# A fused attention and expert kernel: the last block of keys and queries takes another way through PSUM, and its high and low parts are cut in two

## The chip, the cores and the metric

The kernel runs on one core of one Trainium2 chip. The metric is device time in microseconds of one execution, from the first to the last instruction with what lies around them. Engines are named as the profile names them: PE (TensorE matmuls), PEld (its weight loads), DVE (VectorE), ACT (ScalarE), POOL (GpSimd) and SP (SyncE, which issues most DMAs here).

## The reference

Block-causal attention in float32 over 8 batches, 8 heads, 576 positions, head size 64, with blocks of 64 positions; its output, as 4608 tokens of 512 numbers, goes through a two-level router (4 groups of 4 experts, one expert for each token) and the chosen expert's two layers.

```python
def _attn_ref(q, k, v):
    scores = np.matmul(q, k.transpose(0, 1, 3, 2)) / sqrt(64)
    scores = where(pos_q // 64 >= pos_k // 64, scores, -1e9)
    attn = softmax(scores)
    return np.matmul(attn, v)

x = attn_out.transpose(0, 2, 1, 3).reshape(4608, 512)
# router: g = argmax(x @ w_group), e = argmax(x @ w_expert[g]), weight = softmax(g) * softmax(e)
# expert: out[token] = weight * (relu(x @ w1[g, e]) @ w2[g, e])
```

## The kernel before

**Attention.** The work is cut into 32 steps, one for each batch and pair of heads. Step i needs the keys and queries of two heads, turned so that the head size lies on the partitions. `prep` (token K) turns the first 512 positions through PE into a PSUM tile, and `full` (k0, k1, on ACT) copies them into the SBUF tile `nf`, 512 columns for k and 512 for q. The last 64 positions of k and q take three small transposes, `flip_last` (line 175), into a second PSUM tile; `full_last` (j0 for k, 64 columns; j1 for q, 128 columns) copies them behind the others in `nf`, on DVE. Scores are computed in two parts of precision, so `nf` is split: `high` (h0 for k, 576 columns; h1 for q, 640 columns, line 194) rounds it into half 0 of the tile `qk`, and `low` (l0, l1, line 199) subtracts that from `nf` into half 1. h0, h1 and l1 run on POOL, l0 on DVE.

**Scores.** `score` (S0 to S3 and S8, line 228 or 218) multiplies high by high, high by low, low by high, in this order. S2 of step i is the first of its step; it does S0's work too, and reads the first 512 columns of k and q alone. S8 is the one that reads the last columns. `rowmax` (D) takes the maxima on DVE, `expo` (E) the exponentials on ACT, `trans` (T) transposes them on PE, t drains these, `values` (V, line 313) multiplies by the values into the PSUM tile `o`, and v on DVE copies that out. All these PSUM tiles come from one pool of four, taken in turn.

**Order.** Every engine runs its instructions in the order in which the program issues them, and that order is written out by hand as the string `ORDER`: one pass over it is a period, and `S2@0` means S2 of step x in period x, `j0@-1d` means j0 of step x+1, on DVE (a: ACT or POOL). In the kernel before, V of step x-2 also takes the three small transposes of step x+1 into its own PSUM tile `o`, behind its products. In the string V is the 21st of 60 tokens, j0, j1, h0, v, D1, l0, D8 and then h1, l1 follow, and S2 of the next step is the third token of the next period. In the first eight periods five further places in the order (one after every 12 tokens) take a DMA issue on POOL: the odd periods use the first, third and fifth, the even ones the second and fourth.

**Experts.** After the attention come the experts, 14 slots with loaded weights and the tokens gathered by index (lines 927 to 1170). `store` scales each finished tile of outputs by the routing weight and scatters its rows into the output by an indirect DMA on POOL (line 1167). In the last slot of the order the scaling is shared: 256 columns on ACT (line 1160), 256 on DVE (line 1161). Behind all slots stands a loop, `overflow` (line 1342), over a count `cnti` that is zero when no expert has more tokens than planned; all engines load the count and test it. The count is written by DVE in `spill` (line 646), at about 519 us.

Of the kernel before, what the change touches and what calls it, by code (L numbers as in the profile page):

```python
# [50 lines left out]

ORDER, ON_DVE = parse("""
Z2@7 E3@1 S2@0 D2@0 Z4@8 E2@1 n1@3a E8@1 T1@1 t3@1a t1@1a D0@0 K@-1 Z0@10 Y1@4 S3@0 D3@0 G2@6 R0@3
k0@-1a V@2 k1@-1a E0@0 E4@0 E5@0 E1@0 M1@4 E6@0 T2@1 S1@0 L0@3 E7@0 t2@1a T4@1 Z3@8 G1@5 S8@0 G0@4 j0@-1d G4@6
j1@-1d t0@1a Z1@9 h0@-1a v@2d L1@2 D1@0 l0@-1d D8@0 n0@3a G3@6 X0@4 X1@5 Y0@3 h1@-1a t4@1a M0@3 l1@-1a T3@0
X2@6
""")

# [9 lines left out]
class Attention:  # L68
# [99 lines left out]

    def flip_last(self, i, ps):

        x = self.lds[i]["k"]
        for z, n in ((0, 0), (1, 0), (1, 1)):
            r = slice(64 * z, 64 * z + 64)
            o = 384 * z + 64 * n
            self.nc.tensor.transpose(out=ps[:, z, o:o + 64], in_=x[r, 8 + 2 * n:10 + 2 * n, :].rearrange("p a d -> p (a d)"),
                                     identity=self.c["ident"][r, r])

# [5 lines left out]
    def full_last(self, i, n):  # L183
        r = self.rs[i]
        w = 64 + 64 * n
        self.evac(("j", n), r["nf"][:, S * n + 512:S * n + 512 + w], r["jps"][:, n, 384 * n:384 * n + w], 0.125 if n else None)

    def side(self, tok):
        return self.nc.vector if tok in self.on_dve else self.nc.gpsimd

    def high(self, i, n, eng=None):
        r = self.rs[i]
        o = slice(S, 2 * S + BLK) if n else slice(0, S)
        (eng or self.side(("h", n))).tensor_copy(r["qk"][:, 0, o], r["nf"][:, o])  # L194

    def low(self, i, n, eng=None):
        r = self.rs[i]
        o = slice(S, 2 * S + BLK) if n else slice(0, S)
        (eng or self.side(("l", n))).tensor_tensor(out=r["qk"][:, 1, o], in0=r["nf"][:, o], in1=r["qk"][:, 0, o].bitcast(F32),  # L199
                                              op=ALU.subtract)  # L200

    PROD = ((0, 0), (0, 1), (1, 0))

    def score(self, i, u):
        nc = self.nc
        r = self.rs[i]
        b, pr = divmod(i, 4)
        if b not in self.sms:
            self.sms[b] = self.small.tile([P, 4, 2, NT], F32, tag="sm", name=f"sm{b}")
            nc.gpsimd.memset(self.sms[b], 1.0)  # L210
        if "nm" not in r:
            r["nm"] = self.small.tile([P, NB], F32, tag="nm", name=f"nm{i}")
        t = r["qk"]
        ps = self.wide(f"s{i}_{u}")
        if u == 8:
            for h in range(2):
                for x, (hq, hk) in enumerate(self.PROD):
                    nc.tensor.matmul(ps[:, h, 0:288], lhsT=t[:, hq, S + 512:S + 512 + P],  # L218
                                     rhs=t[:, hk, 288 * h:288 * h + 288], start=x == 0, stop=x == 2)
            r["s", u] = ps[:, :, 0:288]  # L220
            return
        for u, c0 in ((2, 0), (0, 384)) if u == 2 else ((u, 0),):
            w = P * (u + 1)
            st = r["s", u] = ps[:, :, c0:c0 + w]
            for x, (hq, hk) in enumerate(self.PROD):
                for z in range(2):
                    p = slice(64 * z, 64 * z + 64)
                    nc.tensor.matmul(st[:, z, :], lhsT=t[p, hq, S + P * u:S + P * u + P], rhs=t[p, hk, 0:w],  # L228
                                     start=x == 0 and c0 == 0, stop=False)
        m = 2 if u == 0 else 1  # L230
        for z in range(2):
            p = slice(64 * z, 64 * z + 64)
            o = ps[:, z, c0 + w - P * m:c0 + w].rearrange("p (n c) -> p n c", c=P)[:, :, BLK:]
            nc.tensor.matmul(o, lhsT=self.mq[p, :], rhs=self.mk[p, 0:m, :], start=False, stop=True)  # L234

    def rowmax(self, i, u):
        r = self.rs[i]
# [52 lines left out]
    def values(self, i, N):  # L290
        nc = self.nc
        o = self.wide(f"o{i}")
        if i + 3 < N:
            self.rs.setdefault(i + 3, {})["jps"] = o
        if i >= 0:
            self.products(i, o)
        if i + 3 < N:
            self.flip_last(i + 3, o)

    def products(self, i, o):  # L300
        nc = self.nc
# [22 lines left out]
    def start(self, N, order, on_dve, init):  # L324
        nc = self.nc
        self.load(0)
        self.wsb = self.pb[0][:, 0:256].bitcast(BF16)
        nc.vector.memset(self.wsb, 0.0)
        self.wps = self.wide("wps")[:, 0, :]
        self.warm(7)  # L330
        if N > 1:
            self.load(1)
        init()
        self.clear()
        self.on_dve = set()
        self.prep(0)
        self.on_dve = {("k", 1), ("j", 1)}
        self.values(-3, N)
        for n in range(2):
            self.full(0, n)  # L340
            self.full_last(0, n)
        self.on_dve = on_dve
        self.warm(5)
        self.high(0, 0, nc.vector)
        self.high(0, 1)
        self.low(0, 0, nc.vector)
        self.low(0, 1, nc.vector)
        if N > 2:
            self.load(2)

# [18 lines left out]

    def token(self, i, tok, N):  # L370
        k = tok[0]
        if not (-2 if k == "V" else k in "Kkjhl") <= i < N:
            return
        if k == "S":
            self.score(i, tok[1])
        elif k == "D":
            self.rowmax(i, tok[1])
        elif k in "tv":
            self.drain(i, tok)
        elif k == "E":  # L380
            self.expo(i, tok[1])
        elif k == "T":
            self.trans(i, tok[1])
        elif k == "V":
            self.values(i, N)
        elif k == "K":
            self.prep(i)
        elif k == "k":
            self.full(i, tok[1])
        elif k == "j":  # L390
            self.full_last(i, tok[1])
        elif k == "h":
            self.high(i, tok[1])
        elif k == "l":
            self.low(i, tok[1])
        elif i % 4 == 3:
            self.router.token(self, i // 4, tok)

# [7 lines left out]
R = 64  # L406
# [18 lines left out]
class Router:  # L425
# [184 lines left out]
        self.res = res  # L610
        yield

    def spill(self, at, row, cnti):
        nc = self.nc
        V = nc.vector
        ts, tt, stt = self.ts, self.tt, self.stt
        one = [R, 1]
        x = tt(self.res[:, 1:2], self.cap, ALU.subtract, sh=one)
        xi = self.t(one, I32)
        ts(x, 0.0, ALU.max, P // UNIT - 1.0, ALU.add, out=xi)  # L620
        xi = ts(xi, (P // UNIT).bit_length() - 1, ALU.arith_shift_right, sh=one, dt=I32)
        ov = self.t(one)
        V.tensor_copy(ov, xi)
        st = stt(self.cap, float(UNIT), self.res[:, 2:3], ALU.mult, ALU.add, sh=one)
        rhs = self.t([R, 4, R])
        ts(self.trif, ov[:, 0:1], ALU.mult, out=rhs[:, 0:2, :])
        ts(self.c["ident"][0:R, 0:R], self.res[:, 0:1], ALU.mult, out=rhs[:, 2, :])
        ts(self.c["ident"][0:R, 0:R], st[:, 0:1], ALU.mult, out=rhs[:, 3, :])
        yield
        ps = at.psT("spill")  # L630
        nc.tensor.matmul(ps[0:R, 0:4 * R], lhsT=self.onesf, rhs=rhs.rearrange("p c r -> p (c r)"),
                         start=True, stop=True)
        yield
        g = self.t([R, 4, R])
        V.tensor_copy(g, ps[0:R, 0:4 * R].rearrange("p (c r) -> p c r", r=R))
        lo = ts(g[:, 1, :], self.pid[:, 0:1], ALU.is_le, sh=[R, R])
        ind = stt(g[:, 0, :], self.pid[:, 0:1], lo, ALU.is_gt, ALU.mult, sh=[R, R])
        stt(g[:, 1, :], -128.0, g[:, 3, :], ALU.mult, ALU.add, out=g[:, 3, :])
        ts(g[:, 3, :], self.p128[:, 0:1], ALU.add, out=g[:, 3, :])
        yield  # L640
        prod = tt(g[:, 2:4, :], ind.unsqueeze(1).broadcast_to([R, 2, R]), ALU.mult, sh=[R, 2, R])
        res = self.red(prod, sh=[R, 2])
        col = self.t([R, 2], I32)
        V.tensor_copy(col, res)
        nc.sync.dma_start(row, col)
        V.tensor_copy(cnti[0:1, 0:1], g[0:1, 0, R - 1:R])
        yield

    def token(self, at, b, tok):
# [193 lines left out]
class Moe:  # L843
# [302 lines left out]
    def store(self, s, c, full):  # L1146
# [10 lines left out]
                nc.vector.scalar_tensor_tensor(out=tmp[0:n], in0=y[z:z + n], scalar=cw[z:z + n], in1=src[0:n],  # L1157
                                               op0=ALU.mult, op1=ALU.add)
        elif s.get("o") == len(self.slots) - 1:
            nc.scalar.activation(ys[0:n, 0:256], y[0:n, 0:256], AF.Copy, scale=cw[0:n])  # L1160
            nc.vector.tensor_scalar(out=ys[0:n, 256:512], in0=y[0:n, 256:512], scalar1=cw[0:n], scalar2=None, op0=ALU.mult)
        elif c % 2 == 0:
            nc.vector.tensor_scalar(out=ys[0:n], in0=y[0:n], scalar1=cw[0:n], scalar2=None, op0=ALU.mult)  # L1163
        else:
# [197 lines left out]
def attention_moe(ctx, tc, q, k, v, w_group, w_expert, w1, w2, out, order=None, on_dve=None):  # L1362
# [16 lines left out]
    with tc.manual_schedule(engines={ET.PE, ET.Activation, ET.DVE, ET.Pool, ET.SP}):  # L1379
# [52 lines left out]
            6: [lambda: b("X", 4), lambda: moe.getids(slots[1])],  # L1432
            7: [moe.grow_raw],
        }
        spl = ro.spill(at, rowo, cnti)
        for n in (60, 63, 65, 67, 68, 69):
            hooks[n] = [lambda: next(spl, None)]
        run = moe.run(hooks)
# [21 lines left out]
        b("G", 1)  # L1460
        for _ in run:
            pass
    moe.overflow(cnti, rowo)


# [24 lines left out]
```

## Time and profile before

| what | us |
| --- | --- |
| median of three runs | 786.62 (786.08 to 788.21) |
| the profiled execution, its own time | 785.75 |
| span of that execution in the profile | 784.0 |
| attention, from the start to about | 322 |
| PE busy over the span | 759.1 |

The span is what the instruction records cover; the profiled execution's own time has 1.75 us more around it. The profile's views used below are its page, the list of waits, the timeline of one engine in a stretch, the groups of instructions by line and shape, and the view of one source line. A line of a timeline gives the start in us, the duration in us, the engine, the line of the program, the operation, the tiles (out<-in), the shape, and in brackets how long the engine had been idle and what ended that.

### The profile page before, as it was taken

How to read it: one execution, taken by the hardware profiler on the slowest of the kernel's cores; microseconds unless marked ns; L12 is line 12 of the kernel's file. 1: busy time of each engine (PE TensorE's matmuls, PEld its weight loads, DVE VectorE, ACT ScalarE, POOL GpSimd, SP SyncE). 2: the span in 40 equal slices, each digit the busy share in tenths (PEclk: the TensorE clock that was granted, in tenths of full speed). 3: DMA queues.
4: the chain of work that ended last, by engine and by line, in shares of the span. 5: the costliest groups of instructions: out<-in, count | busy, mean ns of one | idle time of the engine just before them, and what ended most of it. 6: DMA issues, size and time to landing. Idle time of an engine off the chain costs nothing.

```text
span 784.0 us, 20180 instructions
## 1 busy us (share of the span) xinstructions
PE 759.1 (97%) x7422; PEld 620.5 (79%) x7422; DVE 544.7 (69%) x1153; ACT 500.4 (64%) x1244; POOL 350.2 (45%) x481
## 2 busy tenths in 40 slices
PE   7899999999999999999999999999999999999996
PEld 4677777777777787768888788788988888888874
DVE  5567888888888888885454654754666667777742
ACT  5999999999999998755433433432434545545622
POOL 6444345454545454344143644454551553544212
PEclk9999999999999999999999999999999999999999
DMA  6478464646464636443779979979778897787771
GB/s 137 96 210 237 116 137 109 139 109 139 108 139 108 140 102 159 166 123 117 271 203 225 365 228 237 287 223 219 245 200 234 267 268 188 204 250 231 261 245 42
DMA packets 219108, 146.71 MB, mean 187 GB/s; under 512 B 155558, under 2 KB 186870, under 8 KB 219008
## 3 DMA queue, kind: packets, MB, share of 16 engines
q1 hardware_dynamic: 209920, 120.76, 57.6%
q0 software_dynamic: 9088, 24.64, 9.9%
q8 instruction: 60, 0.98, 0.5%
q14 instruction: 40, 0.33, 0.1%
HBM read 113.46 MB, written 24.59 MB: 176 GB/s over the span
## 4 chain that ended last, share of the span: by engine, by line
PE 80%; ACT 7%; DVE 6%; issue 3%; POOL 2%; DMA 2%; POOLq 0%; SPq 0%; ACTq 0%; DVEq 0%
PE h L1050 18%; PE y L1114 18%; PE o L313 10%; PE s L228 7%; PE tp L157 6%; PE h L1043 4%; PE s L218 3%; ACT pb L251 3%; PE ye L1114 3%; ACT pt L284 3%; PE he L1050 3%; PE y L1122 2%; DVE wl L949 1%; PE y L1133 1%; PE lg L690 1%
## 5 line engine op out<-in xcount | busy, mean ns | idle before, releaser
L1050 PE MATMUL h<-xt,wh 128*128 128x264 f32 (+6 forms) x704 | 156.3, 312 | 2.4 <-DVE xt L1010 2.3
L251 ACT ACTIVATE pb<-s,nm 128x128 f32<-128x128 f32 (+4 forms) x288 | 156.1, 568 | 3.5 <-DVE nm L239 1.6
L949 DVE TENSOR_TENSOR wl<-raw,wh 128x512 fp32r<-128x512 f32 x192 | 147.3, 804 | 8.5 <-ACT wh L948 8.4
L239 DVE TENSOR_REDUCE nm<-s 128x2 f32<-128x768 f32 (+4 forms) x160 | 126.3, 806 | 34.1 <-PE s L234 29.9
L1050 PEld LDWEIGHTS h<-xt,wh 128*128 128x128 f32 x704 | 119.2, 188 | 18.2 <-issue 4.2
L948 ACT CAST wh<-raw 128x512 fp32r<-128x512 f32 x192 | 109.6, 618 | 8.6 <-DMA raw<-in_moe_w_dram 6.0
L284 ACT COPY pt<-tp 128x1024 f32<-128x1024 f32 (+4 forms) x160 | 105.3, 696 | 8.6 <-PE tp L157 6.4
L1050 PE MATMUL h<-xt,wl 128*128 128x264 f32 (+6 forms) x352 | 109.2, 310 | 0.0
L1114 PE MATMUL y<-wh,hring 128*128 128x512 f32 x306 | 106.9, 400 | 0.4 <-ACT ys L1165 0.2
L228 PE MATMUL s<-qk 64*128 64x384 f32 (+3 forms) x768 | 89.9, 343 | 6.4 <-POOL qk L199 3.0
L1167 POOL DMA_INDIRECT out_dram<-ys,ids x40 | 47.0, 1174 | 108.1 <-DVE ys L1163 88.3
L313 PE MATMUL o<-pt,vb 128*64 128x320 f32 (+4 forms) x896 | 93.6, 360 | 0.4 <-DVE tmp L708 0.2
L194 POOL CAST qk<-nf 128x640 fp32r<-128x640 f32 (+1 forms) x63 | 42.7, 701 | 98.1 <-DVE nf L281 71.4
L313 PEld LDWEIGHTS o<-pt,vb 128*64 128x64 f32 x896 | 59.3, 137 | 32.2 <-DVE tmp L708 0.3
L157 PE MATMUL tp<-ident,pb 64*128 64x64 f32 x1600 | 76.3, 226 | 1.6 <-DVE xT L281 1.1
L228 PEld LDWEIGHTS s<-qk 64*128 64x128 f32 x768 | 61.6, 188 | 15.0 <-POOL qk L199 6.1
L157 PEld LDWEIGHTS tp<-ident,pb 64*128 64x128 f32 x1600 | 63.8, 140 | 10.2 <-ACT pb L251 3.9
L982 POOL COPY pl<-xg 128x1024 int16<-128x1024 int16 (+3 forms) x35 | 40.3, 1154 | 62.3 <-DMA xg<-xd,ids 40.6
L1114 PEld LDWEIGHTS y<-wh,hring 128*128 128x128 f32 x306 | 57.4, 188 | 13.1 <-DVE hring L1061 0.5
L1050 PEld LDWEIGHTS h<-xt,wl 128*128 128x128 f32 x352 | 66.2, 188 | 1.2
L251 ACT ACTIVATION_READ_ACCUMULATOR pb<-s,nm 128x1 f32 x288 | 64.1, 223 | 0.0
L199 POOL TENSOR_TENSOR qk<-nf,qk 128x640 fp32r<-128x640 f32 x31 | 61.2, 1975 | 2.6
(255 smaller groups left out, 1324.0 us busy)
## 6 DMA issues: line engine op xcount, KB each, us to landing
raw<-in_moe_w_dram SPq DMA_DIRECT2D x96, 512.0 KB, 4.2
rawq<-in_moe_w_dram SPq DMA_DIRECT2D x24, 512.0 KB, 7.8
natk<-in_k_dram SPq DMA_DIRECT2D x32, 256.0 KB, 3.6
natq<-in_q_dram SPq DMA_DIRECT2D x32, 256.0 KB, 5.5
vb<-in_v_dram SPq DMA_DIRECT2D x64, 128.0 KB, 2.8
wh<-in_moe_w_dram SPq DMA_DIRECT2D x16, 512.0 KB, 5.0
xd<-xns SPq DMA_DIRECT2D x12, 512.0 KB, 3.2
tab<-fill POOLq DMA_DIRECT2D x10, 512.0 KB, 4.1
```

Source lines behind the costliest of these rows:

```text
L157: self.nc.tensor.transpose(out=out[:, z], in_=src[r], identity=self.c["ident"][r, r])
L199: (eng or self.side(("l", n))).tensor_tensor(out=r["qk"][:, 1, o], in0=r["nf"][:, o], in1=r["qk"][:, 0, o].bitcast(F32), op=ALU.subtract)
L228: nc.tensor.matmul(st[:, z, :], lhsT=t[p, hq, S + P * u:S + P * u + P], rhs=t[p, hk, 0:w], start=x == 0 and c0 == 0, stop=False)
L239: self.nc.vector.tensor_reduce(out=o, in_=r["s", u], op=ALU.max, axis=ax, negate=True)
L251: nc.scalar.activation(reg, src, AF.Exp, bias=r["nm"][:, t:t + 1], accum_out=self.sms[b][:, pr, z, u:u + 1])
L284: return self.nc.scalar.copy(dst, src)
L313: nc.tensor.matmul(o[64 * a:64 * a + 64, hf, c0:c0 + BLK * (b1 - t)], lhsT=r["v"][:, a, j, :], rhs=pt[:, PTJ * j + t:PTJ * j + b1, a, :], ...
L948: nc.scalar.copy(h[:, sl], s["raw", u][:, sl])
L949: nc.vector.tensor_tensor(out=l[:, sl], in0=s["raw", u][:, sl], in1=h[:, sl].bitcast(F32), op=ALU.subtract)
L1050: nc.tensor.matmul(o, lhsT=ww[:, dc, f], rhs=rr[:, dc, t], start=dc == 0 and x == 0, stop=dc == 3 and x == 2)
L1114: nc.tensor.matmul(y[c][0:n], lhsT=hh, rhs=w, start=k == 0 and x == 0, stop=k == 7 and x == 2)
L1167: i = nc.gpsimd.indirect_dma_start(out=self.out, out_offset=bass.IndirectOffsetOnAxis(ap=s["ids"][0:n, c, 0:1], axis=0), in_=ys[0:n], in_o ...
```

## The change

- V no longer takes the three small transposes. S1 of step x takes those of step x+1, behind its own products, into columns 256 to 383 of each half of its score tile, which S1 (256 columns wide) leaves unused. For the first step they go into a tile of their own.
- high and low are cut into the first 512 columns and the last ones (kt, 64 columns of k; qt, 128 columns of q). h0 is now one instruction over the first 512 columns of k and of q together (1024 columns), right behind k1 in the order. h1 is two small ones, kt and qt. l0 is low of k's first 512 columns, on DVE; l1 is low of q's first 512 columns, on POOL; a new l2 is low of kt and qt, on POOL.
- In the order, j0 and j1 stand behind D1 instead of ahead of v; h1 stands right behind them, then l0 and D8; l1 keeps its place and l2 comes two tokens behind it.
- In the last slot ACT scales all 512 columns. The count of the overflow loop is copied into `cnti` by POOL at the very end of the experts' work instead of by DVE in `spill`.

```diff
-k0@-1a V@2 k1@-1a E0@0 E4@0 E5@0 E1@0 M1@4 E6@0 T2@1 S1@0 L0@3 E7@0 t2@1a T4@1 Z3@8 G1@5 S8@0 G0@4 j0@-1d G4@6
-j1@-1d t0@1a Z1@9 h0@-1a v@2d L1@2 D1@0 l0@-1d D8@0 n0@3a G3@6 X0@4 X1@5 Y0@3 h1@-1a t4@1a M0@3 l1@-1a T3@0
+k0@-1a V@2 k1@-1a h0@-1a E0@0 E4@0 E5@0 E1@0 M1@4 E6@0 T2@1 S1@0 L0@3 E7@0 t2@1a T4@1 Z3@8 G1@5 S8@0 G0@4 G4@6
+t0@1a Z1@9 v@2d L1@2 D1@0 j0@-1d j1@-1d h1@-1a l0@-1d D8@0 n0@3a G3@6 X0@4 X1@5 Y0@3 l1@-1a t4@1a M0@3 l2@-1a T3@0
...
+        self.rs.setdefault(i, {})["jps"] = ps
...
-            o = 384 * z + 64 * n
+            o = 256 + 64 * n
...
+    def part(self, t, n):
+
+        if n == "kq":
+            return t[:, 0:2 * S].rearrange("p (n c) -> p n c", c=S)[:, :, 0:512]
+        return t[:, dict(k=slice(0, 512), q=slice(S, S + 512), kt=slice(512, S), qt=slice(S + 512, 2 * S + BLK))[n]]
...
+        eng.tensor_copy(self.part(r["qk"][:, 0], n), self.part(r["nf"], n))
...
+        eng.tensor_tensor(out=self.part(r["qk"][:, 1], n), in0=self.part(r["nf"], n),
+                          in1=self.part(r["qk"][:, 0], n).bitcast(F32), op=ALU.subtract)
...
+        if u == 1 and i + 1 < self.N:
+            self.flip_last(i + 1, ps)
...
-        if i + 3 < N:
-            self.rs.setdefault(i + 3, {})["jps"] = o
-        if i >= 0:
-            self.products(i, o)
-        if i + 3 < N:
-            self.flip_last(i + 3, o)
+        self.products(i, o)
...
-            self.high(i, tok[1])
+            for n in ("kt", "qt") if tok[1] else ("kq",):
+                self.high(i, n, self.side(tok))
         elif k == "l":
-            self.low(i, tok[1])
+            for n in (("k",), ("q",), ("kt", "qt"))[tok[1]]:
+                self.low(i, n, self.side(tok))
...
-        V.tensor_copy(cnti[0:1, 0:1], g[0:1, 0, R - 1:R])
+        self.over = g[0:1, 0, R - 1:R]
...
-            nc.scalar.activation(ys[0:n, 0:256], y[0:n, 0:256], AF.Copy, scale=cw[0:n])
-            nc.vector.tensor_scalar(out=ys[0:n, 256:512], in0=y[0:n, 256:512], scalar1=cw[0:n], scalar2=None, op0=ALU.mult)
+            nc.scalar.activation(ys[0:n], y[0:n], AF.Copy, scale=cw[0:n])
...
+        nc.gpsimd.tensor_copy(cnti, ro.over)
     moe.overflow(cnti, rowo)
```

## Rows read from the trace of the kernel before

**Rows 1.** The page: busy us (share of the span) and instructions of each engine.
```profile
PE 759.1 (97%) x7422; PEld 620.5 (79%) x7422; DVE 544.7 (69%) x1153; ACT 500.4 (64%) x1244; POOL 350.2 (45%) x481
```

**Rows 2.** The list of waits, whole span: us in total, times, longest us.
```profile
PE s L228 <- POOL qk L199: 3.0, 4, 1.0
...
PEld s L228 <- POOL qk L199: 6.1, 13, 1.3
```

**Rows 3.** Timeline of DVE, 198 to 203 us: j0, j1, v, D1, l0.
```profile
198.72 0.23 DVE L281 COPY nf<-o 128x64 f32<-128x64 f32 x1 [0.18 <-PE o L175]
198.86 0.28 DVE L282 TENSOR_SCALAR nf<-o 128x128 f32<-128x128 f32 x1
199.06 0.75 DVE L281 COPY xT<-o 128x576 f32<-128x576 f32 x1
199.72 0.68 DVE L239 TENSOR_REDUCE nm<-s 128x2 f32<-128x512 f32 x1
200.32 0.75 DVE L199 TENSOR_TENSOR qk<-nf,qk 128x576 fp32r<-128x576 f32 x1
```

**Rows 4.** Timeline of POOL, the same stretch: h0 and h1 (merged), l1.
```profile
199.08 1.32 POOL L194 CAST qk<-nf 128x576 fp32r<-128x576 f32 x2 [0.49 <-DVE nf L281]
200.49 1.99 POOL L199 TENSOR_TENSOR qk<-nf,qk 128x640 fp32r<-128x640 f32 x1
```

**Rows 5.** Timeline of PE, the same stretch: T4 begins, S1 ends, S8, S2.
```profile
199.41 0.25 PE L157 MATMUL tp<-ident,pb 64*128 64x64 f32 x1
199.43 0.20 PE L234 MATMUL s<-mk,mq 64*128 64x64 bf16 x1
...
199.95 1.03 PE L218 MATMUL s<-qk 128*128 128x288 f32 x6
...
202.01 1.25 PE L228 MATMUL s<-qk 64*128 64x384 f32 x12
```

**Rows 6.** Timeline of POOL, then of PE, 109.5 to 114.8 us: l1, T4, S8, S2.
```profile
111.68 2.11 POOL L199 TENSOR_TENSOR qk<-nf,qk 128x640 fp32r<-128x640 f32 x1
...
111.40 0.53 PE L157 MATMUL tp<-ident,pb 64*128 64x64 f32 x10
111.85 1.05 PE L218 MATMUL s<-qk 128*128 128x288 f32 x6
...
113.86 1.06 PE L228 MATMUL s<-qk 64*128 64x384 f32 x12
```

**Rows 7.** Timeline of all engines, 20 to 26 us: an l1 and the l0 that overlaps it.
```profile
22.47 1.54 POOL L199 TENSOR_TENSOR qk<-nf,qk 128x640 fp32r<-128x640 f32 x1
...
23.09 1.53 DVE L199 TENSOR_TENSOR qk<-nf,qk 128x576 fp32r<-128x576 f32 x1
```

**Rows 8.** Groups by line and shape, POOL, 0 to 320 us: xcount | busy us, mean ns | idle before.
```profile
L194 POOL CAST qk<-nf 128x576 fp32r<-128x576 f32 x31 | 20.6, 664 | 96.3 <-DVE nf L281 71.4 <-ACT pb L251 24.9
...
L667 POOL COPY ry<-rx 128x20 f32<-128x20 f32 x14 | 2.3, 195 | 26.7 <-DVE rx L664 26.7
```

**Rows 9.** Timeline of POOL, 51 to 56 us: an early period, between h0 and h1.
```profile
52.34 0.53 POOL L515 DMA_DIRECT2D tab<-fill  x1
```

**Rows 10.** Timelines at the end: ACT 766 to 769 us, then all engines from 775 us.
```profile
767.83 0.69 ACT L1165 ACTIVATE ys<-y,ids 128x512 f32<-128x512 f32 x1 [1.51 <-DVE ys L1163]
...
776.97 0.47 ACT L1160 ACTIVATE ys<-y,ids 128x256 f32<-128x256 f32 x1 [4.94 <-PE y L1114]
778.02 0.48 DVE L1161 TENSOR_SCALAR ys<-y,ids 128x256 f32<-128x256 f32 x1 [5.27 <-ACTq L1342]
778.79 0.99 POOL L1167 DMA_INDIRECT out_dram<-ys,ids  x1 [5.81 <-DVE ys L1161]
```

**Rows 11.** Lines 1342 and 1486: xcount: duration ns min/median/max, first and last start us.
```profile
L1342 PEldq EVENT_SEMAPHORE  x13: 51/51/51, 777.0 to 778.7; - x13
L1342 POOLq INC_SWDGE_SEM  x1: 943/943/943, 773.5 to 773.5; - x1
...
L1486 POOLq DRAIN  x3: 46/115/4631, 778.6 to 783.7; - x3
```

More of the change, by code (lines that the diff above doesn't have):

```diff
@@ L185, in full_last, with high, low @@
         w = 64 + 64 * n
-        self.evac(("j", n), r["nf"][:, S * n + 512:S * n + 512 + w], r["jps"][:, n, 384 * n:384 * n + w], 0.125 if n else None)
+        self.evac(("j", n), r["nf"][:, S * n + 512:S * n + 512 + w], r["jps"][:, n, 256:256 + w], 0.125 if n else None)
     def side(self, tok):
         return self.nc.vector if tok in self.on_dve else self.nc.gpsimd
-    def high(self, i, n, eng=None):
+    def part(self, t, n):
+        if n == "kq":
+            return t[:, 0:2 * S].rearrange("p (n c) -> p n c", c=S)[:, :, 0:512]
+        return t[:, dict(k=slice(0, 512), q=slice(S, S + 512), kt=slice(512, S), qt=slice(S + 512, 2 * S + BLK))[n]]
+    def high(self, i, n, eng):
         r = self.rs[i]
-        o = slice(S, 2 * S + BLK) if n else slice(0, S)
-        (eng or self.side(("h", n))).tensor_copy(r["qk"][:, 0, o], r["nf"][:, o])
-    def low(self, i, n, eng=None):
+        eng.tensor_copy(self.part(r["qk"][:, 0], n), self.part(r["nf"], n))
+    def low(self, i, n, eng):
         r = self.rs[i]
-        o = slice(S, 2 * S + BLK) if n else slice(0, S)
-        (eng or self.side(("l", n))).tensor_tensor(out=r["qk"][:, 1, o], in0=r["nf"][:, o], in1=r["qk"][:, 0, o].bitcast(F32),
-                                              op=ALU.subtract)
+        eng.tensor_tensor(out=self.part(r["qk"][:, 1], n), in0=self.part(r["nf"], n),
+                          in1=self.part(r["qk"][:, 0], n).bitcast(F32), op=ALU.subtract)
     PROD = ((0, 0), (0, 1), (1, 0))
@@ L337, in start @@
         self.on_dve = {("k", 1), ("j", 1)}
-        self.values(-3, N)
+        self.N = N
+        self.flip_last(0, self.wide("jp"))
         for n in range(2):
@@ L343, in start @@
         self.warm(5)
[L344 to L347, printed above, removed]
+        self.high(0, "k", nc.vector)
+        self.high(0, "q", nc.gpsimd)
+        self.low(0, "k", nc.vector)
+        self.low(0, "q", nc.vector)
+        for n in ("kt", "qt"):
+            self.high(0, n, nc.gpsimd)
+        for n in ("kt", "qt"):
+            self.low(0, n, nc.gpsimd)
         if N > 2:
@@ L371, in token @@
         k = tok[0]
-        if not (-2 if k == "V" else k in "Kkjhl") <= i < N:
+        if not 0 <= i < N:
             return
@@ L611, in final, with spill @@
         yield
-    def spill(self, at, row, cnti):
+    def spill(self, at, row):
         nc = self.nc
@@ L1434, in attention_moe @@
         }
-        spl = ro.spill(at, rowo, cnti)
+        spl = ro.spill(at, rowo)
         for n in (60, 63, 65, 67, 68, 69):
```

## The prediction

> **What bounds the kernel now.** The page comes first: PE is busy for 759.1 of 784.0 us [rows 1], so anything that does not make PE wait less, or do less, moves little. The change takes no work from PE: the three small transposes go from V to S1, one for one. What is left is the 25 us in which PE waits, and the list of waits says which of them the change can touch. PE waits for the low part of q from POOL (l1) 17 times in 31 periods: 13 times as a weight load, 6.1 us in all, and 4 times as a matmul, 3.0 us [rows 2]. All other changes of the attention touch waits of tenths.
>
> Then the timelines of one period show why l1 is late. DVE copies j0 and j1 at 198.72 and 198.86, then v, D1 and l0 [rows 3]. POOL runs h0 and h1 from 199.08 to 200.40 and l1 from 200.49 to 202.48 [rows 4]. S2 of the next step starts at 202.01, and its third product is the first that needs l1 [rows 5]. Its twelve matmuls take 1.25 us there, against 1.06 us in a period where l1 was done before S2 began, at 113.79 against 113.86 [rows 6]. So PE and POOL are nearly balanced: in 13 of the later periods l1 comes out just too late and costs PE up to 0.19 us, in the others it has about 0.4 us in hand (the first four matmuls need no l1). A period repeats through this chain: S2 waits for l1, the rest of PE's period follows, and out of it come the next transposes. Whatever l1 loses in those 13 periods, the kernel loses each time.
>
> The end of the kernel is the second place: ACT's half of the last scaling starts at 776.97, DVE's half only at 778.02, after ACT's part of the overflow loop's test, and the last scatter at 778.79 [rows 10].
>
> **The chain of l1, before and after.** The anchor is D1, which waits for the end of S1. S1's last matmul ends at 199.63 [rows 5]; D1 starts at 199.72, right behind v [rows 3]. Without the transposes PE gets to S1 about 0.15 us sooner, an estimate from ten transposes in 0.53 us [rows 6], and at its end it spends about that again on them. The tracking of PSUM goes by tile, so D1 waits for them too: I put its start 0.04 us earlier, no more. v is done by then, 0.5 us sooner than now. So D1 stays where it is, and j0 and j1, which ran ahead of it, now run behind it.
>
> Before, from D1's start to l1's end: 202.48 - 199.72 = 2.76 us.
>
> After, counted from D1's start: j0 at 0.60 (as l0 followed D1, 199.72 to 200.32), j1 at 0.74 (0.14 behind j0), l0 at 0.94 (0.20 behind j1, as v was) [rows 3]. l0 has 512 columns in place of 576: 0.75 x 512 / 576 = 0.67, to 1.61. kt needs j0 to have landed, qt needs j1: j0's end at 198.95 was followed by h0 at 199.08 [rows 3, 4], so kt can start at 0.95 and meets l0.
>
> Here the two engines hinder each other. Where l1 ran first, alone, it took 1.54 us, and l0, started in the middle of it at 23.09, ended at 24.62, 0.62 us behind l1's end at 24.01: it took 1.53 us in place of 0.75 [rows 7, 3]. Where l0 ran first, to 201.07, l1 took 1.99 us and ended 1.41 us behind it [rows 3, 4]. One waits for the other's end, and only its start-up, some 0.13 us, is hidden. The Trainium skill has this as a rule (SBUF — State Buffer, Who interferes with whom): VectorE with two SBUF inputs and a GpSimd instruction that reads SBUF exclude each other for a whole instruction, and the one that starts first goes first. The rows agree, 1.99 against 1.54 us; by the rule alone the order of kt and l0 here is open, since both could start at about 0.95.
>
> The prices of kt and qt are in no row. Below them stands a copy of 20 columns, 195 ns; above them h0's 576 columns, 664 ns [rows 8]. Between the two lies 0.84 ns a column, so kt is 0.23 us and qt 0.29 us. Behind l0 kt adds 0.10 (its start is hidden), qt 0.24 (POOL's instructions overlap by 0.05). l1 has 512 columns: 1.41 x 0.8 + 0.13 = 1.26, less 0.05 of overlap, 1.21. Its end: 1.61 + 0.10 + 0.24 + 1.21 = 3.16. GPSIMD Engine Reference of the Trainium skill (Elementwise — side-by-side cycle accounting) gives 4497 ns for 2048 columns of such an instruction, from which I estimate 1.12 us for l1; by that the sum below would be lower by 16 x 0.14 = 2.2 us, and no row has that size.
>
> So l1 ends 3.16 - 0.04 - 2.76 = 0.36 us later than now. It is shorter by 128 columns and h0 is out of its way, but it had been behind l0 and not behind h0 all along, and l0 and the small high parts now start behind D1 and both copies. Bounds: if kt, qt, l0 and l1 did not hinder each other at all, l1 would end at 1.02 (j1's end) + 0.13 + 0.24 + 1.26 = 2.65, which is 0.15 earlier than now. If l0 came last, behind kt, qt and l1, it would end at 2.65 + 0.62 = 3.27; S2's second product needs it about 0.15 before the third needs l1, so PE would wait for it as if l1 were 0.65 later.
>
> **The sum.** 13 periods x 0.36 = 4.7 us. Of the four waits as a matmul, all in the first periods, I count three at the same 0.36, 1.1 us; the first of them falls in step 0, where PE has other waits beside it, and I take 0 (0.36 more if they do not cover it). A DMA issue of 0.53 us that stood between h0 and h1 in the even early periods [rows 9] now stands, by the order, between h1 and l1, so it delays l1 as before. The other 11 later periods have their 0.4 us in hand and lose nothing.
>
> h0 over 1024 columns costs POOL about 0.2 + 0.84 x 1.0 = 1.04 us, right behind k1. Its result is needed by S2 of the next step, after V, T2, S1, T4, S8 and T3, and POOL is idle in most of that time (busy 350.2 of 784.0 us [rows 1]), so it costs nothing; without that cover it would be 1 us. l2, some 0.7 us, comes behind l1 and is needed by S8 half a period on: nothing. v ends 0.5 us sooner, and S8, which started 0.14 us behind v's end and 0.54 behind T4's first transpose, 0.45 where v is not in its way [rows 3, 5, 6], gains up to 0.09; in the 13 periods l1 decides anyway, elsewhere I take 0.4 us in all off. At the start the low part of q is 128 columns shorter on DVE: 0.1 off. Moving the next loads behind S1 delays only transfers that are needed more than a period later: nothing.
>
> The end: ACT's whole scaling takes 0.69 (as at 767.83), to 777.66, and 0.28 later, as now, the scatter starts: 777.94 in place of 778.79, 0.85 sooner [rows 10]. But POOL's copy of the count now stands behind that scatter's issue of 0.99, and every engine's test of the loop behind the copy. PE's part of the test took from 777.0 to 778.7, and POOL has a step of 0.94 in its own [rows 11]; all of that lay beside the last scaling and would now come after 779.0, up to about 782.7. The last drain on POOL ended at 783.2 (778.55 + 4.63) [rows 11], so it ends between 0.85 us earlier (if it hangs on the scatter alone) and 2.9 us later (if its 3.4 us behind the scatter's issue come after the test). I take 0.2 off, because the test fits in what the drain waits for now.
>
> Together: 4.7 + 1.1 - 0.4 - 0.1 - 0.2 = 5.1 us. The profiled execution took 785.75 us, 1.75 more than its span, and lies 0.87 below the median of 786.62. On the median this is 791.7 us.
>
> **Rivals.** (a) l0 comes last on its port: kt starts a moment before l0 and POOL keeps its turn. For it speaks that kt and l0 become ready within 0.02 us; against it that l0 came on right behind the one POOL instruction that held it up, with 0.62 us left [rows 7]. 13 x 0.65 + 3 x 0.65, and about 0.1 in the 11 others: 786.6 + 11 = 798 us. (b) Faster: kt and qt slip through ahead of l0 without holding it or l1 up, and l1 ends 0.15 us earlier. It decides from the point where l1 ends less than 2.76 us behind D1. Then 13 x 0.15 = 2.0, three early ones 0.5, S8 up to 0.8, 0.3 at both ends: 783.0 us. For it speaks that POOL's chain gets 1.3 us of h0 and h1 off; against it that j0 and j1 come 1.6 us later. (c) The change does not do what it is for, and nothing shows: kt and qt cost half of what I think, l1 ends within 0.1 of now, and PE's time for a period decides: 786 to 788 us. (d) The loop's test at the end sets the time, with the chain as forecast: 791.7 + 3 = 794.8 us.
>
> **How the numbers follow.** Measurements here tell differences from about 0.3%, 2.4 us, so "same" is 784.3 to 789.0. Chances: forecast 0.45, (d) with it 0.08, (a) 0.12, (c) 0.19, (b) 0.16. Faster is (b), 0.16; same is (c), with 0.02 of the forecast's lower tail, 0.21; slower the rest, 0.63. The forecast's own range, with l1 at 2.2 us less or kt and qt twice as dear, is 789 to 795. The 8 in 10 leave out half of (b) below and some of (a) above: 783.6 to 797.
>
> **What would show it.** In the profile after, per period: l0 on DVE about 0.3 us later against D1; POOL with one cast of about 1.0 us behind k1 and two small ones around l0; l1 about 1.3 us long, its end some 3.1 us behind D1's start. PE's wait for l1 at S2 in more than 17 periods, and 10 us or more in all. Period lengths up by 0.3 to 0.4 in the two of four that are short now, unchanged in the others. At the end, the scatter at about 1 us behind PE's last matmul, and all engines' tests of the loop behind it. I am wrong if l1 ends less than 2.8 us behind D1, if D1 itself moves, or if S2 is seen waiting for l2, which its first 512 columns do not need.

## The result, and the profile after

The median went from 787.07 us (five runs, 786.08 to 788.21) to 792.66 us (five runs, 791.60 to 795.52): 1.0077 times the time before, with a 95% interval of 1.0055 to 1.0099. The kernel became slower by 5.6 us; the forecast was 791.7 us, with a range of 783.6 to 797.0. The profiled execution took 791.6 us and its span 789.9 us, 5.85 us more than the span before.

The page of the kernel after, busy us and instructions of each engine, against [rows 1]:

```profile
PE 757.4 (96%) x7422; PEld 617.5 (78%) x7422; DVE 546.5 (69%) x1151; ACT 502.6 (64%) x1244; POOL 370.0 (47%) x579
```

PE does the same 7422 matmuls, so the added time is PE's waiting or lies behind PE. POOL has 98 instructions and 20 us more. The list of waits says what PE waits for, against [rows 2]:

```profile
PEld s L233 <- POOL qk L204: 14.6, 20, 1.9
...
PE s L233 <- POOL qk L204: 8.3, 18, 1.6
```

S2's weight loads wait for the low part of q 20 times in place of 13 and 8.5 us longer, and its matmuls 18 times in place of 4, in the same periods, 5.3 us longer. One short period shows why. DVE's timeline after, 161 to 166 us (v, D1, j0, j1, l0, D8), against [rows 3]:

```profile
160.82 0.76 DVE L288 COPY xT<-o 128x576 f32<-128x576 f32 x1
162.06 0.69 DVE L246 TENSOR_REDUCE nm<-s 128x2 f32<-128x512 f32 x1 [0.48 <-PE s L176]
162.67 0.21 DVE L288 COPY nf<-s 128x64 f32<-128x64 f32 x1
162.80 0.28 DVE L289 TENSOR_SCALAR nf<-s 128x128 f32<-128x128 f32 x1
163.00 0.73 DVE L204 TENSOR_TENSOR qk<-nf,qk 128x512 fp32r<-128x512 f32 x1
163.65 0.74 DVE L246 TENSOR_REDUCE nm<-s 128x1 f32<-128x576 f32 x1
```

POOL's timeline, the same stretch (kt and qt as one row; l1 and the two parts of l2 as one), against [rows 4]:

```profile
162.95 0.93 POOL L200 CAST qk<-nf 128x64 fp32r<-128x64 f32 x2 [2.21 <-DVE nf L288]
163.85 1.96 POOL L204 TENSOR_TENSOR qk<-nf,qk 128x512 fp32r<-128x512 f32 x3
```

PE's timeline, the same stretch (S8, and S2 in two pieces), against [rows 5, 6]:

```profile
162.26 1.05 PE L223 MATMUL s<-qk 128*128 128x288 f32 x6
...
164.29 0.61 PE L233 MATMUL s<-qk 64*128 64x384 f32 x4
165.18 0.72 PE L233 MATMUL s<-qk 64*128 64x384 f32 x8 [0.27 <-POOL qk L204]
```

D1 waits 0.48 us for S1's tile, now with the small transposes in it; j0 and j1 follow, then l0. Of the merged row of POOL the single records give kt from 162.95 to 163.18, qt from 163.14 to 163.88, 0.15 behind l0's end, and l1 from 163.85 to 165.12. So l1 ends 3.06 us behind D1's start, 0.30 later than the 2.76 before. PE's third product waits for it and goes on 0.06 behind it. From V's start l1 ends at 7.27 us in place of 6.99, and the short periods are longer by just that, 0.28 us.

Groups of POOL by line and shape, 0 to 322 us, in the kernel after (count, busy us, mean ns, idle before), against [rows 8]:

```profile
L204 POOL TENSOR_TENSOR qk<-nf,qk 128x512 fp32r<-128x512 f32 x31 | 39.4, 1271 | 0.0
L200 POOL CAST qk<-nf 128x1024 fp32r<-128x1024 f32 x31 | 32.1, 1036 | 35.4 <-ACT nf L292 35.4
L200 POOL CAST qk<-nf 128x128 fp32r<-128x128 f32 x32 | 23.7, 740 | 0.0
...
L200 POOL CAST qk<-nf 128x64 fp32r<-128x64 f32 x32 | 8.6, 268 | 72.0 <-DVE nf L288 72.0
```

The end, in a timeline of all engines after 775 us, against [rows 10]:

```profile
780.09 0.69 ACT L1169 ACTIVATE ys<-y,ids 128x512 f32<-128x512 f32 x1 [4.94 <-PE y L1123]
781.05 0.99 POOL L1175 DMA_INDIRECT out_dram<-ys,ids  x1 [4.95 <-ACT ys L1169]
782.03 0.18 POOL L1471 CAST cnti<-fin 1x1 int32<-1x1 f32 x1
```

and in the views of the lines of the loop and of the end (count, ns min/median/max, first and last start), against [rows 11]:

```profile
L1349 POOLq TENSOR_LOAD <-cnti x1: 773/773/773, 782.2 to 782.2; - x1
...
L1350 POOLq INC_SWDGE_SEM  x1: 975/975/975, 783.4 to 783.4; - x1
...
L1495 POOLq DRAIN  x3: 46/109/3257, 785.8 to 789.6; - x3
```

All engines load the count at 782.2, behind its copy, and POOL's last step of the test starts at 785.6. Only then does POOL's drain begin, and it takes 3.26 us of its own, though the scatter's instruction had ended at 782.04, 3.7 us before. Before, the drain began at 778.55 and ran beside the scatter.

Where the 5.85 us lie, by the starts of V's products (from one to the next is a period) and the end of PE's last matmul. From the sixth on, the periods come in fours: two short ones, one of a third kind and one of a fourth.

| stretch | before | after | difference |
| --- | --- | --- | --- |
| start to the first V | 28.69 | 27.83 | -0.86 |
| the first five periods | 49.17 | 50.41 | +1.24 |
| 12 short periods (9.32 before, 9.60 after) | 111.88 | 115.26 | +3.38 |
| 6 periods of the third kind (10.2; 10.1) | 61.25 | 60.59 | -0.66 |
| 5 periods of the fourth kind (10.4) | 52.46 | 53.36 | +0.90 |
| the last three | 25.15 | 25.16 | 0.0 |
| last V to PE's last matmul | 448.33 | 447.45 | -0.88 |
| PE's last matmul to the end | 7.09 | 9.82 | +2.73 |

The first row and the last but one are not put down to the change, since kernels with the same code there differ by as much: the first V starts at 28.69 to 29.59 in the kernel before and in experiments 2 and 8, at 27.83 and 28.82 in the kernel after and in experiment 1, and the stretch from the last V to PE's last matmul is 447.5 to 451.7 us over the ten profiles of this study.

Of the +0.90 of the fourth kind 0.60 lies in one period, which took 10.93 us before and 11.53 after. POOL's timeline there in the kernel after, then DVE's:

```profile
270.03 1.05 POOL L200 CAST qk<-nf 128x1024 fp32r<-128x1024 f32 x1
...
270.16 0.94 DVE L539 TENSOR_TENSOR fin<-fin,eb 64x16 f32<-64x16 f32 x1
```

The router's small addition ends 0.02 us behind h0, and v stands behind it on DVE. Before, with POOL idle there, it took 0.15 us. All seven kernels of this study with h0 over 1024 columns show 0.94 us there, the three with the old h0 0.15.

### The profile page after: what moved, and what is told of

Its sections match the earlier page's. It is cut to its first block, busy times and chain, and to the rows that moved or that the text cites. A ratio compares the mean times of both kernels' runs of the same rounds, so it can differ in the third digit from the quotient of the medians.

```text
span 789.9 us, 20222 instructions
## 1 busy us (share of the span) xinstructions
PE 757.4 (96%) x7422; PEld 617.5 (78%) x7422; DVE 546.5 (69%) x1151; ACT 502.6 (64%) x1244; POOL 370.0 (47%) x579
## 4 chain that ended last, share of the span: by engine, by line
PE 75%; ACT 8%; DVE 7%; POOL 5%; issue 3%; DMA 1%; SPq 0%; DVEq 0%; ACTq 0%
PE h L1059 19%; PE y L1123 18%; PE o L315 11%; PE s L233 7%; PE tp L157 6%; PE h L1052 4%; ACT pt L291 3%; PE ye L1123 3%; ACT pb L258 3%; POOL qk L204 3%; PE he L1059 3%; PE y L1131 2%; POOL qk L200 2%; DVE wl L958 2%; DVE nm L246 2%
## 5 line engine op out<-in xcount | busy, mean ns | idle before, releaser
L958 DVE TENSOR_TENSOR wl<-raw,wh 128x512 fp32r<-128x512 f32 x192 | 148.9, 813 | 7.0 <-ACT wh L957 6.8
L200 POOL CAST qk<-nf 128x128 fp32r<-128x128 f32 (+3 forms) x96 | 63.8, 679 | 109.1 <-DVE nf L288 72.0
L233 PEld LDWEIGHTS s<-qk 64*128 64x128 f32 x768 | 59.7, 188 | 20.2 <-POOL qk L204 14.6
L157 PEld LDWEIGHTS tp<-ident,pb 64*128 64x128 f32 x1600 | 61.5, 139 | 14.0 <-ACT pb L258 5.9
L204 POOL TENSOR_TENSOR qk<-nf,qk 128x64 fp32r<-128x64 f32 (+2 forms) x95 | 61.8, 675 | 0.0
```

Source lines behind the costliest of these rows:

```text
L157: self.nc.tensor.transpose(out=out[:, z], in_=src[r], identity=self.c["ident"][r, r])
L200: eng.tensor_copy(self.part(r["qk"][:, 0], n), self.part(r["nf"], n))
L204: eng.tensor_tensor(out=self.part(r["qk"][:, 1], n), in0=self.part(r["nf"], n), in1=self.part(r["qk"][:, 0], n).bitcast(F32), op=ALU.subtract)
L958: nc.vector.tensor_tensor(out=l[:, sl], in0=s["raw", u][:, sl], in1=h[:, sl].bitcast(F32), op=ALU.subtract)
```

## The experiments

Ratios are to the kernel before on the same chip, with 95% intervals. Experiments 5 to 8 ran on another chip than 1 to 4.

**1. The count early again.** The kernel after, with the count copied by DVE in `spill` as before; ACT alone in the last slot stays.

```diff
+        V.tensor_copy(self.cnti, self.over)
...
-        nc.gpsimd.tensor_copy(cnti, ro.over)
```

> The changed kernel, but with the overflow count written by DVE in the router's spill, as before; ACT scales the last slot alone, as in the changed kernel. Theory A (the loss has two parts: the low part of q, some 4 us, and the loop's test behind the last scatter, 2.8 us): 789 to 790 us, the last 9.8 us behind PE's last matmul shrink to 6.3 to 7.1. Theory B (the forecast's: the end costs nothing, the whole loss is in the attention): 792 to 793, as the changed kernel.

Measured: 791.06 us, 1.0049 (1.0030 to 1.0067). From PE's last matmul to the end 7.02 us in place of 9.82: the late count costs the end 2.8 us. The median is only 1.6 us below that of the kernel after, and the profile's span, 790.6 us, is no shorter: its first period took 11.65 us in place of 10.35, with the same code. So the 2.8 us are read from the end alone.

**2. The end's two edits alone.** The kernel before, with ACT alone in the last slot and the late count.

```diff
-        V.tensor_copy(cnti[0:1, 0:1], g[0:1, 0, R - 1:R])
+        self.over = g[0:1, 0, R - 1:R]
...
+            nc.scalar.activation(ys[0:n], y[0:n], AF.Copy, scale=cw[0:n])
...
+        nc.gpsimd.tensor_copy(cnti, ro.over)
```

> The kernel before with the change at the end alone: ACT scales the last slot by itself and POOL copies the count at the very end. Theory A: 2 to 2.8 us slower than before, about 789.5, all of it behind PE's last matmul. Theory B: 0.2 us faster than before, 786.8. Both: the attention as before.

Measured: 789.22 us, 1.0030 (1.0018 to 1.0042); from PE's last matmul to the end 9.81 us, the periods as before. Its end, in the timeline, and in the view of the last line:

```profile
778.41 0.99 POOL L1166 DMA_INDIRECT out_dram<-ys,ids  x1 [4.95 <-ACT ys L1160]
779.38 0.18 POOL L1462 CAST cnti<-fin 1x1 int32<-1x1 f32 x1
```

```profile
L1486 POOLq DRAIN  x3: 46/109/3257, 783.1 to 786.9; - x3
```

The same drain of 3257 ns begins 4.7 us behind the scatter's start. So the end's share of the slowdown is shown by itself: 2.7 us against the kernel before (9.81 for 7.09), and 2.4 by the ratio.

**8. ACT alone.** The kernel before, with ACT's scaling of all 512 columns in the last slot and nothing else.

```diff
-            nc.scalar.activation(ys[0:n, 0:256], y[0:n, 0:256], AF.Copy, scale=cw[0:n])
-            nc.vector.tensor_scalar(out=ys[0:n, 256:512], in0=y[0:n, 256:512], scalar1=cw[0:n], scalar2=None, op0=ALU.mult)
+            nc.scalar.activation(ys[0:n], y[0:n], AF.Copy, scale=cw[0:n])
```

> The kernel before, with the last slot scaled by ACT alone and nothing else changed. Theory A (the late count is the whole loss at the end): same as before within 0.5 us; the end 7.0 to 7.1 us behind PE's last matmul, because the scatter still stands behind the loop's test. Theory E (the scaling by ACT alone is a gain that the late count eats): 0.8 us faster at the end.

Measured: 786.34 us, 0.9998 (0.9986 to 1.0010); from PE's last matmul to the end 7.01 us, against 7.09 before. Its timeline at the end:

```profile
777.35 0.69 ACT L1160 ACTIVATE ys<-y,ids 128x512 f32<-128x512 f32 x1 [4.94 <-PE y L1114]
779.10 0.99 POOL L1166 DMA_INDIRECT out_dram<-ys,ids  x1 [5.74 <-issue]
```

ACT is done at 778.04, but the scatter starts 1.06 later, behind POOL's own steps of the test: with the count early, these stand ahead of the scatter (its sequencer's last branch there begins at 778.2). So half a scaling less gains next to nothing; and in the kernel after, where the scatter does come 0.28 behind ACT, the test comes behind it.

**3. l1 right behind h0.** The kernel after, with l1 moved in the order to the place right behind h0, so that it does not queue behind kt and qt.

```diff
-k0@-1a V@2 k1@-1a h0@-1a E0@0 ... X0@4 X1@5 Y0@3 l1@-1a t4@1a
+k0@-1a V@2 k1@-1a h0@-1a l1@-1a E0@0 ... X0@4 X1@5 Y0@3 t4@1a
```

> The changed kernel with one token moved: l1, the low part of q's first 512 columns, stands right behind h0 in the order, ahead of j0, j1 and the small high parts, in place of behind them. The same instructions on every engine. Theory A (the loss in the attention is l1's place behind D1, both copies and the small parts): PE's wait for l1 at S2 is gone in every period, 7 to 10 us faster than the changed kernel, 783 to 786, and 2.8 us of the end still in it. Theory C (the loss is POOL's greater load, or the transposes' new place on PE): within 1.5 us of the changed kernel, 791 to 794.

Measured: 794.80 us, 1.0096 (1.0073 to 1.0120): no faster than the kernel after, a miss. S2 no longer waits for l1, which is 2.5 to 5.7 us ahead, and short periods take 9.37 us. But the third kind takes 11.00 to 11.08 in place of 10.1. The timeline of this kernel there, POOL, DVE and PE:

```profile
177.25 1.27 POOL L204 TENSOR_TENSOR qk<-nf,qk 128x512 fp32r<-128x512 f32 x1
...
177.40 1.95 DVE L778 TENSOR_TENSOR pre<-pre,o 128x16 bf16<-128x16 bf16 x5
...
180.13 0.72 DVE L288 COPY xT<-o 128x576 f32<-128x576 f32 x1
...
180.99 1.03 PE L223 MATMUL s<-qk 128*128 128x288 f32 x6 [0.93 <-DVE xT L288]
```

and the same five additions of the router in the kernel after:

```profile
178.78 0.97 DVE L778 TENSOR_TENSOR pre<-pre,o 128x16 bf16<-128x16 bf16 x5
```

The early l1 holds up the router's five small additions, 1.95 us in place of 0.97: the single records give the first of them 1.14 us, to 0.02 behind l1's end, and the other four 0.17 each. v comes behind them on DVE, and S8, whose PSUM tile is one of the same four, waits for v. The wait for l1 was turned into a wait for v.

**4. The pieces alone.** The kernel before, with high and low cut in pieces, but V's transposes, the shared scaling and the early count as before, and j0, j1 and h1 ahead of v.

```diff
-k0@-1a V@2 k1@-1a E0@0 ... j1@-1d t0@1a Z1@9 h0@-1a v@2d L1@2 D1@0 l0@-1d D8@0 ... h1@-1a t4@1a M0@3 l1@-1a T3@0
+k0@-1a V@2 k1@-1a h0@-1a E0@0 ... j1@-1d t0@1a Z1@9 h1@-1a v@2d L1@2 D1@0 l0@-1d D8@0 ... l1@-1a t4@1a M0@3 l2@-1a T3@0
```

> The kernel before with the pieces alone: h0 over 1024 columns behind k1, h1, l0, l1, l2 cut as in the change, but the transposes stay in V, j0 and j1 stay ahead of v, and h1 takes h0's old place ahead of v; the end as before. Theory A: l1 ends about 0.9 us before S2 needs it in all periods; faster than before by 2 to 5 us, 782 to 785. Theory C (POOL's load): no faster than before, 787 or more.

Measured: 788.36 us, 1.0018 (1.0007 to 1.0029): a miss again. l1 now has 1.7 to 2.3 us in hand, and yet short periods take 9.30 us, against 9.32. Timelines of a short period, of DVE (D1, l0, D8), then of ACT and PE:

```profile
131.17 0.68 DVE L243 TENSOR_REDUCE nm<-s 128x2 f32<-128x512 f32 x1
131.77 0.97 DVE L203 TENSOR_TENSOR qk<-nf,qk 128x512 fp32r<-128x512 f32 x1
132.66 0.74 DVE L243 TENSOR_REDUCE nm<-s 128x1 f32<-128x576 f32 x1
```

```profile
134.23 1.00 ACT L288 COPY pt<-tp 128x1024 f32<-128x1024 f32 x1
```

```profile
133.46 1.07 PE L232 MATMUL s<-qk 64*128 64x384 f32 x12
...
134.93 0.42 PE L157 MATMUL tp<-ident,natq 64*128 64x64 f32 x8
135.29 0.50 PE L232 MATMUL s<-qk 64*128 64x512 f32 x2
```

S2 is 0.18 shorter than in [rows 5], as it should be. But l1 ran from 130.90 to 132.19 and now holds l0 up, which takes 0.97 us; D8 stands behind l0, ACT's exponentials of D8 behind it, and ACT's drain of the transposes behind those. S3 starts 0.05 us behind that drain. Counted from V's start, D8 comes at 5.73 us and S3 at 8.36, against 5.53 and 8.40 before: of the 0.2 us only 0.04 is left. In the third kind, 10.4 in place of 10.2, S8 waits for v six times. The wait for l1 had become one for l0, by way of D8 and ACT.

**5. The copies ahead of D1.** The kernel after, with j0, j1 and h1 ahead of D1, l0 behind D1 still.

```diff
-t0@1a Z1@9 v@2d L1@2 D1@0 j0@-1d j1@-1d h1@-1a l0@-1d D8@0
+t0@1a Z1@9 v@2d L1@2 j0@-1d j1@-1d h1@-1a D1@0 l0@-1d D8@0
```

> The changed kernel with j0, j1 and h1 ahead of D1 in the order; l0 stays behind D1. Theory A (the loss in the attention comes from what stands between the end of S1 and l1: D1, both copies, l0 on the shared port, the small parts): j0 starts 0.6 us sooner against the end of S1, but l0 now falls on l1 and one of them waits for the other; the short periods 9.4 to 9.5 us in place of 9.60, 2 to 3 us faster than the changed kernel. Theory C (the place of the copies does not matter; the small parts on POOL do): short periods 9.60, no change.

Measured: 813.01 us, 1.0339 (1.0321 to 1.0356): 20 us slower than the kernel after, where it was expected to be faster. The timeline shows POOL's l1, then DVE's l0 and D8, and PE's T3 in a short period:

```profile
172.67 2.43 POOL L204 TENSOR_TENSOR qk<-nf,qk 128x512 fp32r<-128x512 f32 x3
...
172.86 1.64 DVE L204 TENSOR_TENSOR qk<-nf,qk 128x512 fp32r<-128x512 f32 x1
...
174.42 0.74 DVE L246 TENSOR_REDUCE nm<-s 128x1 f32<-128x576 f32 x1
...
176.14 0.46 PE L157 MATMUL tp<-ident,pb 64*128 64x64 f32 x8 [0.62 <-ACT pb L258]
```

l1 does end 1.69 us behind D1's start, 1.37 sooner than after (D1 itself starts 0.34 later, behind the copies). But it starts 0.19 us ahead of l0, and l0 then takes 1.64 us in place of 0.73. D8 stands behind l0 on DVE, ACT's exponentials behind D8, and PE's transposes behind those. From its list of waits, PE for ACT's exponentials and for l0 (the kernel after has 6.2 us in 9 waits in the first of the two groups):

```profile
PEld tp L157 <- ACT pb L258: 20.2, 33, 1.1
...
PEld s L233 <- DVE qk L204: 7.4, 18, 1.6
```

Every kind of period between the first five and the last three is 0.4 to 0.7 us longer in the mean (short ones 10.27), and the first five together 5.4. This is what rival (a) describes, l0 last, brought about by another order, and it costs more than its sum said, since that counted only S2's wait for l0 and not D8 behind l0.

**6. l0 ahead of D1.** The kernel after, with one token moved: l0 right behind v.

```diff
-t0@1a Z1@9 v@2d L1@2 D1@0 j0@-1d j1@-1d h1@-1a l0@-1d D8@0
+t0@1a Z1@9 v@2d l0@-1d L1@2 D1@0 j0@-1d j1@-1d h1@-1a D8@0
```

> The changed kernel with l0 directly behind v on DVE, ahead of D1, where DVE has 0.5 us idle; j0, j1 and the small parts stay behind D1. Theory A with the port: kt, qt and l1 run on POOL alone, l1 ends about 2.65 us behind D1's start in place of 3.06, D1 starts up to 0.2 us later; short periods 9.30 to 9.40, PE's wait for l1 nearly gone, 3 to 5 us faster than the changed kernel. Theory D (the port costs nothing here; POOL's own work and the late copies are all): l1 ends 2.9 us or more behind D1, short periods 9.5 to 9.6.

Measured: 789.98 us, 1.0039 (1.0027 to 1.0052), 2.7 us below the kernel after by the medians, 3.0 by the ratios. DVE's timeline of this kernel in a short period, then POOL's:

```profile
159.35 0.68 DVE L204 TENSOR_TENSOR qk<-nf,qk 128x512 fp32r<-128x512 f32 x1
159.95 0.68 DVE L246 TENSOR_REDUCE nm<-s 128x2 f32<-128x512 f32 x1
160.55 0.21 DVE L288 COPY nf<-s 128x64 f32<-128x64 f32 x1
160.68 0.28 DVE L289 TENSOR_SCALAR nf<-s 128x128 f32<-128x128 f32 x1
```

```profile
160.83 0.48 POOL L200 CAST qk<-nf 128x64 fp32r<-128x64 f32 x2 [2.22 <-DVE nf L288]
161.28 1.98 POOL L204 TENSOR_TENSOR qk<-nf,qk 128x512 fp32r<-128x512 f32 x3
```

l0 runs in the time in which D1 had waited for S1's tile. kt and qt together take 0.48 in place of 0.93, l1 ends 2.61 us behind D1's start in place of 3.06, and short periods take 9.19 in place of 9.60. The first five periods together take 47.5 us in place of 50.4. Part of it is given back: the third kind takes 10.43 to 10.52, not 10.1, because D1 is later there and PE waits 0.60 to 0.70 us for ACT's exponentials in place of 0.18. From the first V to the last the profile is 5.4 us shorter than that of the kernel after, more than the medians say. In the profile the start is 1.8 us longer, and so is, by 4.3, the stretch from the last V to PE's last matmul, whose code did not change; why is not shown.

**7. Both.** The kernel after, with l0 behind v, then j0, j1, h1, and D1 behind them, and the count early.

```diff
-t0@1a Z1@9 v@2d L1@2 D1@0 j0@-1d j1@-1d h1@-1a l0@-1d D8@0
+t0@1a Z1@9 v@2d l0@-1d L1@2 j0@-1d j1@-1d h1@-1a D1@0 D8@0
```

> Both moves together (v, l0, j0, j1, h1, D1 in this order) and the overflow count in the spill as before. Theory A: short periods 9.30, the third kind of period 10.1 (v early), the end 7.1 us behind PE's last matmul; 784 to 786.5 us, 0.1 to 0.4% faster than the kernel before. If D1, now up to 0.5 us later, holds the exponentials up, the short periods stay above 9.4 and the kernel is no faster than before.

Measured: 785.72 us, 0.9996 (0.9979 to 1.0012): as before, and not faster. Short periods take 9.10 us, 0.22 less than before: l0 is out of the way of both l1 and D8, which comes 5.51 us behind V's start, and ACT's drain lets S3 go at 8.16; the third kind takes 10.51 to 10.60, some 0.35 more. One row of ACT's timeline and one of PE's show where PE waits in the latter:

```profile
140.16 0.47 ACT L258 ACTIVATE pb<-s,nm 128x256 f32<-128x256 f32 x1 [0.55 <-DVE nm L246]
...
141.23 0.71 PE L157 MATMUL tp<-ident,pb 64*128 64x64 f32 x16 [0.69 <-ACT pb L258]
```

In those periods the router's work on DVE delays v already. What is put between v and D1 delays D1, ACT's exponentials wait for D1, and PE's transposes for the exponentials. (In the later four of the six such periods the view names a step of the router, L815, in place of ACT; that step ends within 0.02 us of the transposes' start, and they read nothing that it writes.) The order is one string for all periods, and no place for l0 was found here that suits both kinds.

## Why the prediction was right

For the attention it was right in its mechanism. In size it was right in part by luck: the step for the end failed by 2.9 us, and this was made up by a term sized 1.3 us too high and by 1.7 us at the start and behind the last V, where kernels with the same code differ by as much.

- **D1 stays.** Forecast 0.04 us earlier; from V's start to D1's it is 4.23 us before and 4.21 after.
- **j0, j1, l0 behind D1.** Forecast at 0.60, 0.74 and 0.94; measured 0.61, 0.74 and 0.94.
- **kt, qt, l1.** kt alone takes about 0.24 and qt 0.30 (experiments 5 and 6), against 0.23 and 0.29. kt started 0.05 us ahead of l0 and was done early, as in rival (b); qt was not and waited for l0, as forecast. l1 takes 1.27, against 1.26 forecast. The prediction's other estimate, 1.12, was too low. l1's end is at 3.06 from D1's start against 3.16, so 0.28 us later than before, with D1's 0.02, and not 0.36. That the one that starts first holds the other up, as the Trainium skill has it (SBUF — State Buffer, Who interferes with whom), is what this trace shows for qt, 740 ns against 0.30 us, and experiment 5 for l0, 1.64 us against 0.68.
- **13 short periods x 0.36 = 4.7.** Measured 12 x 0.28 = 3.4: over-sized by 1.3. The count was a misreading of [rows 2]: of its 13 weight-load waits five lie in the first 65 us, where the four matmul waits lie too and were counted again; only eight are in short periods, and the other four short periods stand in the list under a later instruction of POOL (L812). That the periods follow S2's wait was the right way to sum: experiment 6 takes 0.41 out of a short period by ending l1 0.41 sooner from V's start, which shows the cause.
- **Early periods 1.1, other periods -0.4.** Measured 1.24, and -0.66 with +0.90 in the fourth kind. Of the 0.90, 0.60 lies in one period (10.93 to 11.53), in which PE waits 0.82 us for v in place of 0.48, and 0.23 in another, whose cause stays open. What delays v in the first is h0, the next point.
- **h0 costs nothing.** 1036 ns measured, 1.04 forecast. POOL has the time for it, but DVE does not: in the long period of the fourth kind h0 holds up the router and with it v. This step looked at POOL alone and missed up to 0.6 us.
- **The end, -0.2.** This is the step that failed: "because the test fits in what the drain waits for now". Measured +2.73. The scatter came where it was forecast, 0.28 behind ACT. But the drain's time is not a wait for the scatter alone: 3.26 us of it come behind the last step of the test, though the scatter's instruction had ended 3.7 us before. This was the upper bound (2.9, from 3.4 us behind the test) and rival (d), to which 0.08 was given. Experiments 1, 2 and 8 show it: late count 2.7 to 2.8 us of the end, ACT alone less than 0.1.

With the measured terms the attention gives +4.9 and the end +2.7, 7.6 in all, against 5.1 forecast. The start and the stretch behind the last V were 1.7 shorter in the profiled execution, within what other profiles show too, which leaves 5.85. The ratio's interval, 4.3 to 7.8 us, holds both figures.

What the text did not see is the second limit just behind the first: l0 stands ahead of D8 on DVE, and through ACT's exponentials and drain it sets S3 as l1 sets S2. Experiments 4 and 5 relieve l1, let it run into l0, and lose the gain (4) or far more (5). The medians of the twelve short periods, counted from V's start, show both limits in every kernel. With 1.41 us from l1's end and 2.63 us from D8's start, both fitted to these traces, S3 starts at the later of the two, and the period ends 0.92 to 0.94 us behind S3's start:

| kernel | l1's end + 1.41 | D8's start + 2.63 | S3's start | period |
| --- | --- | --- | --- | --- |
| before | 8.40 | 8.16 | 8.40 | 9.32 |
| after | 8.68 | 8.43 | 8.68 | 9.60 |
| experiment 3 | 4.08 | 8.43 | 8.43 | 9.37 |
| experiment 4 | 6.67 | 8.36 | 8.36 | 9.30 |
| experiment 5 | 7.64 | 9.33 | 9.33 | 10.27 |
| experiment 6 | 8.27 | 8.14 | 8.27 | 9.19 |
| experiment 7 | 7.67 | 8.14 | 8.16 | 9.10 |

So l1 alone sets the loss of 0.28 us, and taking it away alone gives back only 0.23 (experiment 3). Experiment 7 shows what the transposes in S1 and the pieces can offer, 9.10 us in a short period; the order of the kernel after misses it, because l0 waits behind D1, j0 and j1 while DVE stands idle for 0.48 us ahead of D1.

## What to carry to other kernels

Before an instruction is moved on an in-order engine, list what stands behind it there and which instruction of the other engine it may run into: by the medians, moving l0 ahead of D1 was worth -2.7 us, letting l1 start ahead of it +20 us. Put such work where its engine waits for another anyway. Work on an idle engine is not free if it holds up a busy one: POOL's cast of 1.05 us made a DVE addition of 0.15 take 0.94. Work moved behind the last instruction is paid in full if the closing steps begin behind it, even when it looks as if it would run beside a transfer.

## What the hardware showed

- POOL's closing drain takes 3257 ns behind the loop's test in all five kernels with the late count, and begins 4.7 us behind the scatter's start; with the early count it takes 4.62 to 4.64 us and lies beside the scatter. What it still waits for, or does, in those 3257 ns no run here tells; an end without a scatter wasn't tried.
- Even an addition of 16 columns on DVE is held up by what POOL is doing: 1.14 us in place of 0.17 beside its subtraction of 512 columns (experiment 3), 0.94 in place of 0.15 beside its cast of 1024 (kernel after).
- l0 behind a running l1 takes 1.64 us, 0.68 alone; l1 takes 1.28 us in experiment 6 beside D8, a reduction out of PSUM, so that does not hold it up.
